# Folding the first LayerNorm of a transformer block into its projections: raw rows transposed, statistics by TensorE, normalised copies by GpSimd

## The chip, the cores and the metric

The kernel runs on one core of one Trainium2 chip. The metric is the device time of one execution in microseconds (us); several executions are taken and their median is compared. Engines are called PE or TensorE (matmul), DVE or VectorE, ACT or ScalarE, POOL or GpSimd, and SP or SyncE, which here only issues DMAs.

## The reference

One pre-LayerNorm attention block and one gated feed-forward block over 2048 rows of 512 features, in bf16:

```python
x = A_x
h = x + _A_ref(_layernorm(x, axis=-1), A_wqkv, A_wo)
h2 = h + _B_ref(_layernorm(h, axis=-1), B_w_gate, B_w_up, B_w_down)

# _A_ref: 32 heads of 16 features, softmax over all 2048 keys
scores = einsum("bhqd,bhkd->bhqk", q, k) * 16 ** -0.5
o = einsum("bhqk,bhkd->bhqd", softmax(scores), v)
# _B_ref: F = 1792
h = sigmoid(x @ w_gate) * (x @ w_up); return h @ w_down
# _layernorm: (x - mean) / sqrt(var + 1e-5), no gain and no offset
```

## The kernel before, in words

The rows are cut into 16 tiles of 128 (`NT`), which form four chunks of 512 rows (`NQC`, `QC`, four tiles `TQ` each). The 32 heads are cut into eight groups of four (`NG`), two groups to a pair (`NP`). `KT[g]` holds the transposed keys of a group, one head to a quadrant of 32 partitions, with a row that is one in each quadrant; `QT[g]` holds the queries of a chunk with a shift in that row, so that scores come out shifted against overflow. `Vaug` holds the values with a constant column for the softmax sums.

**Head.** Raw rows are loaded into `xb`. For each row tile the mean and variance come from DVE (bn_stats, L133, L136) or from ACT (two activations with accumulators, L221 and L223, then two small fixes on DVE). A square root on ACT and a reciprocal on DVE give `rstd`; DVE writes the normalised rows `xn` (L238), TensorE transposes them (L151), DVE or ACT copies the result into `xnT[c]` (L245). Then group 0 is projected (`proj0`, L250) with padded weights `w0p`; keys go to `KT[0]` (L260, L262), their squares through a matmul to a minimum (`kmin`, L297), and with that the shift of the queries (`QT[0]`, L320). Values of eight row tiles are also made here (L155, L182, L184). The instructions are `Task`s with a duration and dependencies; a list scheduler in the program places them on the engines and so writes each engine's order. Task `go` ends the head.

**Loop.** The work of attention is 2048 units of 128 keys by 512 query columns for one head, or by 256 columns for two. Three units (`GU`) form a tile of three PSUM banks, 683 tiles in all. For every tile TensorE makes the scores (L887). ACT takes the exponential of two or three banks (L1227). Where it takes two, DVE takes the third: a tensor_scalar writes an integer code `J` of the scores (L1054), and three further ones add constants to four such codes at a time (`code`, L1074); read as bf16 they sum to the exponential. TensorE multiplies with the values into `acc` (L1028). A second planner with a clock for each of P, A and D decides in which order the three engines do this and which units DVE takes; it never gives DVE a unit in tiles 10 to 19. Between tiles it fits background work from the queue `bg`: values (`prep_v`), keys and queries (`prep_k`, `prep_q`, `prep_q0`), the output projection, the second LayerNorm, and the feed-forward layers of the halves of 256 rows that are finished. `ones_fill` sets a whole `KT[g]` to ones by a DMA, all seven in the head; `spread` then puts the keys over it.

**Tail.** The last half's output projection, LayerNorm and feed-forward layer run after the last exponential.

Each engine runs its instructions in the order written, and waits on semaphores of the others.

Of the kernel before, what the change touches and what calls it, by code (L numbers as in the profile page):

```python
# [26 lines left out]
def kernel(  # L27
# [41 lines left out]
    otp = ctx.enter_context(tc.tile_pool(name="otp", bufs=12))  # L69
# [6 lines left out]
    onecol = const.tile([P, 1], FP32)  # L76
    sel = const.tile([P, 32], BF16)
    selq = const.tile([P, P], BF16)
    ones = const.tile([P, 128], BF16)
    xnT = [const.tile([P, DC, QC], BF16, name=f"xnT{c}") for c in range(NQC)]  # L80
    KT = [const.tile([P, S], BF16, name=f"KT{g}") for g in range(NG)]
# [5 lines left out]
    o2buf = [const.tile([P, QC // 32, 32], BF16, name=f"o2_{i}") for i in range(4)]  # L87
# [6 lines left out]
    w0s = prep.tile([P, 2, DC, 64], BF16)  # L94
    w0p = prep.tile([P, 2, DC * 4, 32], BF16)
# [3 lines left out]
    for c in range(NQC):  # L99
        n = 1 if c == 0 else 2  # L100
        for i in range(0, TQ, n):
            q = (nc.sync, nc.scalar)[(i // n) % 2]
            q.dma_start(out=xb[c][:, i:i + n, :], in_=x_v[:, c * TQ + i:c * TQ + i + n, :])
        if c == 0:
            nc.sync.dma_start(out=w0s[:, 0], in_=wqkv_v[:, :, D:D + 64])
            nc.scalar.dma_start(out=w0s[:, 1], in_=wqkv_v[:, :, 0:64])
# [5 lines left out]
    nc.gpsimd.memset(Vaug[:, :, :, DH:VW], 0.5)  # L112
# [3 lines left out]
    nc.vector.memset(selq[:], 0.0)  # L116
    nc.vector.memset(ones[:], 1.0)
    nc.vector.memset(w0p[:], 0.0)
    nc.vector.tensor_reduce(out=sel[:, 0:8], in_=ident_bf[:].rearrange("p (r k) -> p r k", k=DH),
                            axis=AX.X, op=ALU.max)  # L120
    nc.vector.tensor_reduce(out=onecol[:], in_=ident_bf[:, DH:P:32], axis=AX.X, op=ALU.max)
    nc.vector.tensor_scalar(out=selq[:, DH:P:32], in0=sel[:, 0:8:2], scalar1=-0.5078125,
                            scalar2=None, op0=ALU.mult)
# [4 lines left out]
    def ones_fill(g):  # L128
        nc.sync.dma_start(out=KT[g][:].rearrange("p (c n) -> p c n", n=P),
                          in_=ones[:].rearrange("p (o n) -> p o n", o=1).to_broadcast([P, NT, P]))  # L130
# [42 lines left out]
    def v_mm(ps, t, a=0, b=DC, mm=quarters):  # L173
        for d in range(a, b):
            mm(ps, xnT[t // TQ][:, d, (t % TQ) * P:(t % TQ + 1) * P], wv_sb[:, d, :],
               d == 0, d == DC - 1)

    def v_out(ps, t, act):
        dst = Vaug[:, t, :, 0:DH]
        src = ps.rearrange("p (h d) -> p h d", d=DH)  # L180
        if act:
            nc.scalar.copy(out=dst, in_=src)  # L182
        else:
            nc.vector.tensor_copy(out=dst, in_=src)  # L184

    ps0ctx = ExitStack()
    ps0 = ps0ctx.enter_context(tc.tile_pool(name="ps0", bufs=8, space=PSUM))
# [6 lines left out]
    mvs = [small.tile([P, TQ, nc.vector.BN_AGGR_DIM], FP32, name="mv") for c in range(NQC)]  # L194
    rstds = [small.tile([P, TQ], FP32, name="rstd") for c in range(NQC)]
    kmin = small.tile([P, NQC], FP32, name="kmin", bufs=1)
# [5 lines left out]
    class Task:  # L202
        def __init__(self, name, deps, opts, bank=0, frees=0):
            self.name, self.deps, self.opts, self.bank, self.frees = name, deps, opts, bank, frees
            self.end = None
            tasks[name] = self
# [6 lines left out]
    ACT_STATS = {(0, 1), (1, 2), (1, 3), (2, 1), (2, 3), (3, 1), (3, 2)}  # L213
    CHUNK_FIRST = (5400, 7300, 0, 0)

    def stats_task(c, i):
        src, mv = xb[c][:, i, :], mvs[c][:, i, :]

        def on_act():
            junk = prep.tile([P, D], BF16, name="junk")  # L220
            A.activation(out=junk[:], in_=src, func=ACT.Identity, scale=1.0 / D,  # L221
                         accum_out=mv[:, 0:1])
# [18 lines left out]
    def turn0(c, i):  # L241
        buf["t", c, i] = transpose4(bank0(), buf["xn", c, i])
# [97 lines left out]
    while left:  # L340
        best = None
        for n in left:
            t = tasks[n]
            ends = [tasks[d].end for d in t.deps]
            if None in ends or t.bank > banks:
                continue
# [1057 lines left out]
```

## Time and profile before

| quantity | value |
|---|---|
| median of 3 runs | 828.01 us (826.25 to 828.6) |
| the profiled execution | 826.86 us, of which the span of the profile is 825.1 |
| granted TensorE clock | 0.995 of full speed |
| first exponential of the loop | at 33.55 us |
| tiles in which ACT takes two banks, three banks | 479, 204 |
| units that DVE takes (`J`) | 478 |
| GpSimd instructions in the loop | 1 |

All times in a profile line are in microseconds from the span's start unless marked ns. A line of the timeline gives start, duration, engine, source line, operation, what is written and read, and the form. A line of the groups gives the count after the x, then busy time and the mean ns of one instruction, then the idle time before them and who ended it. An instruction's record is longer than the distance to the next one where the two overlap in the pipeline: a `J` is 0.681 long and follows the one before after 0.61.

### The profile page before, as it was taken

To read this page: it belongs to the slowest core of one execution; us is meant where nothing else is said; L and a number is where in the kernel's file an instruction comes from. 1 tells how busy PE (TensorE), PEld (TensorE's weight loads), DVE (VectorE), ACT (ScalarE), POOL (GpSimd) and SP (SyncE) were. 2 spreads that over 40 slices of the span, in tenths; PEclk is the share of its full clock that TensorE was granted. 3 is DMA by queue.
4 is the path that set the end of the run, shared out by engine and by line. 5 is a ranking of instruction groups with operands and counts; after the bars stand their busy time and mean duration, and the time that the engine had idled before them with its cause. 6 is when DMAs were issued, how large, how long until landed. Compare 5 with 4: busy or idle time off the path is not lost.

```text
span 825.1 us, 34604 instructions
## 1 busy us (share of the span) xinstructions
PE 751.6 (91%) x15255; PEld 364.5 (44%) x15259; DVE 734.3 (89%) x1415; ACT 779.8 (95%) x804; POOL 3.2 (0%) x8
## 2 busy tenths in 40 slices
PE   4889988887889999999999999999899999999988
PEld 2322223333335344555444444553455455455546
DVE  8849999997999999999989899889999889899972
ACT  6899999998999999999989999999999999989972
POOL 1000000000000000000000000000000000000000
PEclk9999999999999999999999999999999999999999
DMA  9700011015001121122022211220132022134110
GB/s 259 130 2 4 16 34 27 13 31 159 8 16 54 42 82 35 47 82 78 16 74 61 64 36 47 81 78 16 45 104 84 28 80 79 48 98 141 43 39 16
DMA packets 90717, 49.47 MB, mean 60 GB/s; under 512 B 20820, under 2 KB 90120, under 8 KB 90568
## 3 DMA queue, kind: packets, MB, share of 16 engines
q1 hardware_dynamic: 88936, 46.15, 21.1%
q8 instruction: 121, 1.98, 0.9%
q10 hardware_dynamic: 1632, 1.11, 0.4%
q14 instruction: 28, 0.23, 0.1%
HBM read 37.62 MB, written 2.10 MB: 48 GB/s over the span
## 4 chain that ended last, share of the span: by engine, by line
ACT 45%; PE 33%; issue 14%; DVE 7%; DMA 0%; ACTq 0%; DVEq 0%
ACT pt L1227 42%; PE pm L160 11%; PE pss L887 9%; PE acc L1028 9%; DVE J L1054 2%; ACT th L759 2%; PE gu L155 2%; DVE code L1074 1%; PE hp L1369 1%; DVE xs L970 1%; PE b L151 0%; DVE st L133 0%; DMA code<-in_A_x_dram 0%; DVE hT L743 0%; DVE xn L238 0%
## 5 line engine op out<-in xcount | busy, mean ns | idle before, releaser
L1227 ACT ACTIVATE pt<-pss 128x1024 bf16<-128x1024 f32 (+1 forms) x683 | 727.8, 1192 | 9.4 <-PE pss L887 6.6
L1054 DVE TENSOR_SCALAR J<-pss 128x512 uint16<-128x512 f32 x478 | 318.1, 681 | 24.5 <-PE pss L887 22.9
L887 PE MATMUL pss<-QT,KT 32*128 32x256 bf16 (+1 forms) x3712 | 269.5, 284 | 50.4 <-ACT pt L1227 39.6
L1074 DVE TENSOR_SCALAR code<-J 128x2048 uint16<-128x2048 uint16 (+3 forms) x387 | 237.4, 643 | 0.3
L1028 PE MATMUL acc<-pt,Vaug 128*17 128x256 bf16 (+1 forms) x2837 | 219.2, 286 | 2.0 <-ACT pt L1227 0.8
L887 PEld LDWEIGHTS <-KT 32*128 32x128 bf16 x3712 | 84.9, 92 | 251.3 <-ACT pt L1227 128.8
L1028 PE MATMUL acc<-code,Vaug 128*17 128x256 bf16 (+1 forms) x2625 | 186.4, 284 | 0.0
L1028 PEld LDWEIGHTS <-Vaug 128*17 128x17 bf16 x6337 | 139.7, 90 | 97.8 <-issue 82.2
L1028 PE MATMUL acc<-J,Vaug 128*17 128x256 bf16 (+1 forms) x875 | 137.2, 284 | 0.1
L160 PE MATMUL pm<-xnT,wgu 128*32 128x256 bf16 x3136 | 117.6, 275 | 1.6 <-DVE hT L743 0.8
L160 PEld LDWEIGHTS <-wgu 128*32 128x32 bf16 x3136 | 77.6, 96 | 27.2 <-issue 23.5
L160 PE MATMUL pm<-wd,hT 128*32 128x512 bf16 x784 | 56.1, 382 | 0.0
L743 DVE SCALAR_TENSOR_TENSOR hT<-th,pm 128x512 bf16<-128x512 f32 x49 | 33.3, 679 | 10.1 <-PE pm L160 8.8
L759 ACT ACTIVATE th<-pm 128x512 f32<-128x512 f32 x49 | 30.7, 626 | 8.3 <-PE pm L160 7.3
L970 DVE STREAM_TRANSPOSE xs<-acc 128x512 f32<-128x512 f32 x32 | 22.8, 712 | 11.5 <-PE acc L1028 11.3
L160 PEld LDWEIGHTS <-hT 128*32 128x32 bf16 x784 | 16.0, 95 | 19.6 <-issue 13.1
L160 PE MATMUL pm<-xnT,wq_sb 128*32 128x512 bf16 x256 | 20.5, 391 | 0.2 <-DVE kr L566 0.2
L160 PE MATMUL pm<-xnT,wk_sb 128*32 128x512 bf16 x256 | 19.7, 383 | 0.1
L151 PE MATMUL b<-ident_bf,xn 128*128 128x128 bf16 x64 | 6.5, 265 | 12.1 <-DVE xn L238 11.4
L160 PE MATMUL pm<-wo_sb,ot 128*32 128x512 bf16 x224 | 17.2, 382 | 0.1
L946 DVE STREAM_TRANSPOSE ot<-o 128x256 bf16<-128x256 bf16 x32 | 13.6, 433 | 0.1
L604 DVE TENSOR_SCALAR sh<-pm,kcol 8x512 bf16<-8x512 f32 x16 | 11.8, 735 | 1.9 <-PE pm L600 1.7
(126 smaller groups left out, 327.2 us busy)
## 6 DMA issues: line engine op xcount, KB each, us to landing
wgu<-in_B_w_gate_dram SPq DMA_DIRECT2D x49, 256.0 KB
wgu<-in_B_w_up_dram SPq DMA_DIRECT2D x49, 256.0 KB
KT<-ones SPq DMA_DIRECT2D x7, 512.0 KB
out_dram<-ob SPq DMA_DIRECT2D x16, 128.0 KB
QT<-qd SPq DMA_DIRECT2D x116, 16.0 KB
KT<-kd SPq DMA_DIRECT2D x28, 64.0 KB
wd<-in_B_w_down_dram SPq DMA_DIRECT2D x1, 1792.0 KB
xr<-in_A_x_dram SPq DMA_DIRECT2D x14, 128.0 KB
```

The lines of the kernel that those rows point to most:

```text
L155: nc.tensor.matmul(ps, lhsT=lhsT, rhs=rhs, start=start, stop=stop)
L160: nc.tensor.matmul(ps[r, :], lhsT=lhsT[:, r], rhs=rhs, start=start, stop=stop, tile_position=(0, 32 * j), skip_group_check=True)
L604: nc.vector.tensor_scalar(out=sh[:], in0=ps2[0:8, :], scalar1=-0.505, scalar2=kcol[p][:, 0:1], op0=ALU.mult, op1=ALU.add)
L743: nc.vector.scalar_tensor_tensor(out=hT[:, 2 * k:2 * k + 2, :].rearrange("p f q -> p (f q)"), in0=th[:], scalar=1.0, in1=ps, op0=ALU.add, ...
L759: nc.scalar.activation(out=th[:], in_=ps, func=ACT.Tanh, scale=0.5)
L887: mm = nc.tensor.matmul(pss[:, ui, a * w:(a + 1) * w], lhsT=KT[hg[a]][32 * j:32 * j + 32, kt * P:(kt + 1) * P], rhs=(QT0[q] if g == 0 and ...
L946: nc.vector.transpose(out=ot[:], in_=o2[:, i * NB:(i + 1) * NB, :] .rearrange("p b r -> p (b r)"))
L970: j = st["acc"] = dve(630, lambda: nc.vector.transpose(out=xs[:].rearrange("p b r -> p (b r)"), in_=acc[:]), Mark(T["P"]))
L1028: nc.tensor.matmul(acc[32 * j:32 * j + VW, a * w:(a + 1) * w], lhsT=Vaug[:, kt, 4 * hg[a] + j, :], rhs=un.ap[:, a * w:(a + 1) * w], start= ...
L1054: first = nc.vector.tensor_scalar(out=J[:, k, :], in0=src, scalar1=128 * SC * LOG2E, scalar2=float(CODE_BASE), op0=ALU.mult, op1=ALU.add)
L1074: nc.vector.tensor_scalar(out=c, in0=j, scalar1=CODE_STEP[i], scalar2=None, op0=ALU.add)
L1227: ex = nc.scalar.activation(out=pt[:, lo:lo + wa, :], in_=pss[:, lo:lo + wa, :], func=ACT.Exp, scale=SC)
```

## The change

The normalised row is `rstd * (x - mean)`. If every column of a weight is centred (its mean over the 512 features is taken off), the raw row times the centred weight, times `rstd`, is the same projection, and no mean has to be taken off a row. The change uses this:

- Raw rows are transposed as they land, into `xr[c]`, without statistics. Beside the 128 columns of each row tile stand 64 centred key weights of group 0 and a column of 1/512.
- One matmul of `xr` with itself and these columns (`gram`, four steps for a row tile) gives the Gram matrix, whose diagonal is the sum of squares, the keys of group 0, and the row means. DVE takes the diagonal (product with the identity, then a reduction); ACT squares the mean; variance, square root, reciprocal follow.
- Keys, queries and values of group 0 are scaled by `rstd` on eviction (`scale0`, `vscale0`), transposed by TensorE, and evicted into `KT[0]` and `QT[0]`. Key squares are summed on ACT and DVE from the untransposed keys.
- Column means of weights come from a matmul with a matrix of 1/512 (`wmean`). Group 0's weights are centred by DVE, and copied to the other chunks by GpSimd; `wv`, `wk` and `wq` are centred by GpSimd (`center`), four instructions each.
- GpSimd makes the normalised transposed copies `xnT[c]` (`normalise`), four instructions for each chunk; the row factors get there through DRAM and a broadcast (`spread0`, four writes and four reads on SyncE). The later projections use these copies.
- Values of the other 28 heads are made in the loop for all 16 row tiles, from raw rows, and scaled on eviction; none is made in the head.
- Chunk 3 too takes groups 0 and 1 with 512 columns; DVE may take units in tiles 10 to 19; `ones_fill` moves into `prep_k`; the raw transposed rows of chunks 0 to 2 lie in the `KT` of pairs 1 to 3, the row factors of chunks 0 and 1 in `KT[1]`, until these are filled. All later rows of x are issued by SyncE; a third block of weights (`w0s[:, 2]`) is loaded.

The core of the diff:

```diff
-    for c in range(NQC):
-        n = 1 if c == 0 else 2
-        for i in range(0, TQ, n):
-            q = (nc.sync, nc.scalar)[(i // n) % 2]
...
+    nc.scalar.dma_start(out=w0s[:, 2], in_=wqkv_v[:, :, 2 * D:2 * D + 64])
+    for c in range(1, NQC):
+        for i in range(0, TQ, 2):
+            nc.sync.dma_start(out=xb[c][:, i:i + 2, :], in_=x_v[:, c * TQ + i:c * TQ + i + 2, :])
...
+    nc.gpsimd.memset(Vaug[:, :, :, DH:VW], 0.5)
...
-    def v_out(ps, t, act):
...
+    def v_out(ps, t):
+        nc.vector.tensor_scalar(out=Vaug[:, t, 4:H, 0:DH],
+                                in0=ps[:, 0:D - 64].rearrange("p (h d) -> p h d", d=DH),
+                                scalar1=rstd[:, t:t + 1], scalar2=None, op0=ALU.mult)
...
     def turn0(c, i):
-        buf["t", c, i] = transpose4(bank0(), buf["xn", c, i])
+        buf["t", c, i] = transpose4(bank0(), xb[c][:, i, :])
...
+    def gram(c, i):
+        if not i:
+            buf["g", c] = ps0g.tile([P, TQ, 2 * P], FP32, name="g0")[:]
         for d in range(DC):
-            E.matmul(ps, lhsT=w0p[:, which, 4 * d:4 * d + 4, :], rhs=xnT[c][:, d, :],
+            E.matmul(buf["g", c][:, i, 0:P + 65], lhsT=xr[c][:, d, i, 0:P], rhs=xr[c][:, d, i, 0:P + 65],
                      start=(d == 0), stop=(d == DC - 1))
...
+    def diagonal(c, a, b):
...
+        V.tensor_tensor(out=g[:, a:b, :], in0=buf["g", c][:, a:b, 0:P],
+                        in1=ident_bf[:].rearrange("p (o t) -> p o t", o=1).to_broadcast([P, b - a, P]),
+                        op=ALU.mult)
+        V.tensor_reduce(out=buf["ss", c][:, a:b], in_=g[:, a:b, :], axis=AX.X, op=ALU.add)
...
+    def center0():
+        V.tensor_tensor(out=xr[0][:, :, :, P:P + 64],
...
+        for c in range(1, NQC):
+            nc.gpsimd.tensor_scalar(out=xr[c][:, :, :, P:P + 64], in0=xr[0][:, :, :, P:P + 64],
+                                    scalar1=1.0, scalar2=0.0, op0=ALU.mult, op1=ALU.add)
...
+    def center(ps, w, copy):
+        m = prep.tile([P, D], FP32, name="wmean", bufs=2)
+        copy(out=m[:], in_=ps)
+        for d in range(DC):
+            nc.gpsimd.tensor_tensor(out=w[:, d, :], in0=w[:, d, :], in1=m[:], op=ALU.subtract)
+
+    def normalise(c):
+        for d in range(DC):
+            nc.gpsimd.tensor_tensor(out=xnT[c][:, d, :].rearrange("p (i t) -> p i t", t=P),
+                                    in0=xr[c][:, d, :, 0:P], in1=R[c], op=ALU.mult)
...
     def prep_v(t):
-        yield pe(2, pm_new())
+        yield pe(2, pm_new(), WC["v"])
...
     def prep_k(p, groups=(0, 1)):
+        for a in groups:
+            sp_issue(1, T["P"])
+            ones_fill(2 * p + a)
...
-            yield pe(2, pm_new())
+            yield pe(2, pm_new(), XN[c], WC["k"])
...
-        if (len(tl) == GU and not 10 <= n < 20 and len(jq) < 2
+        if (len(tl) == GU and len(jq) < 2
```

## The prediction, before the changed kernel was run

> **What bounds the kernel now.** I read the page first: the share of each engine, then the sums by stage, then the head in order of time.
>
> ```profile
> PE 751.6 (91%) x15255; PEld 364.5 (44%) x15259; DVE 734.3 (89%) x1415; ACT 779.8 (95%) x804; POOL 3.2 (0%) x8
> ```
>
> ScalarE (ACT) is the fullest engine, and GpSimd (POOL) does nothing. An average over the span hides three stages, so the second view is the busy time in three windows: the head up to the first exponential, the attention loop, the tail.
>
> ```profile
> 0.00:33.50 33.50, 19.74 (x125) 10.95 (x127) 27.89 (x90) 24.20 (x57) 2.90 (x7) 1.00 1.08 235
> 33.50:798.50 765.00, 709.50 (x14929) 338.04 (x14928) 697.29 (x1309) 747.84 (x734) 0.30 (x1) 1.00 0.19 54
> 798.50:825.10 26.60, 22.34 (x205) 15.55 (x204) 9.09 (x17) 7.81 (x13) 0.00 (x0) 0.99 0.05 16
> ```
>
> After each window's length come PE, weight loads, DVE, ACT, POOL, then granted clock and DMA. In the loop ACT is idle for 17 of 765 us: whatever delays it there is lost for good. In the head no engine is full; VectorE (DVE, 27.9 of 33.5 us) is nearest, and the chain that ended last runs there through DVE's statistics, normalisation and reductions. The third view is the order of time around the first exponential.
>
> ```profile
> 31.69 0.75 DVE L320 TENSOR_SCALAR QT<-b,kfull 128x512 bf16<-128x512 f32 x1
> ...
> 32.35 0.68 DVE L184 CAST Vaug<-b 128x512 bf16<-128x512 f32 x1
> 33.09 0.61 PE L887 MATMUL pss<-QT,KT 32*128 32x512 bf16 x6 [1.14 <-DVE Vaug L184]
> ...
> 33.55 1.02 ACT L1227 ACTIVATE pt<-pss 128x1024 bf16<-128x1024 f32 x1 [1.89 <-PE pss L887]
> ```
>
> The shifted queries are done at 32.44, then the scores wait out one more value eviction and the loop starts at 33.55. The change rebuilds everything before this line and puts 28 two-input GpSimd instructions behind it (TensorTensor rows; the program shows them). So I read what the trace knows of GpSimd beside VectorE.
>
> ```profile
> 1.25 2.26 POOL L112 MEMSET Vaug<- 128x512 bf16 x1
> 1.62 0.23 DVE L119 TENSOR_REDUCE sel<-ident_bf 128x8 bf16<-128x128 bf16 x1
> ...
> 1.76 0.14 DVE L121 TENSOR_REDUCE onecol<-ident_bf 128x1 f32<-128x4 bf16 x1
> 1.88 1.66 DVE L122 TENSOR_SCALAR selq<-sel 128x4 bf16<-128x4 bf16 x1
> ```
>
> The tensor_scalar touches 4 elements per partition and takes 1.66 us; small ones elsewhere take 0.16 to 0.17 (nt, nv). It ends at 3.54, 0.03 us after the memset at 3.51. Reductions beside the same memset ran at their usual length. Where a DVE instruction reads and writes SBUF alone, it seems to wait for the running GpSimd instruction. The loop's code instructions are of that kind.
>
> ```profile
> L1054 DVE TENSOR_SCALAR J<-pss 128x512 uint16<-128x512 f32 x478 | 318.1, 681 | 24.5 <-PE pss L887 22.9
> ...
> L1074 DVE TENSOR_SCALAR code<-J 128x2048 uint16<-128x2048 uint16 x327 | 214.2, 682 | 0.2
> ```
>
> A J reads PSUM; a code is SBUF to SBUF and does four times the elements in the same time. The one GpSimd instruction of the loop (ones, 0.30 us at 35.18) ran beside a J of 0.69, the usual length.
>
> **The head, part by part.** Removed: 9 bn_stats of 0.66, 7 pairs of ACT statistics (0.63 each plus a 0.19 accumulator read), 16 normalisations of 0.41, 5 squares, 4 reductions of 0.69, 9 value evictions of 0.6 to 0.7, and the wait for statistics before the first transpose, which now starts on raw rows. The seven 512 KB fills of KT also leave the head's DMA. Added: Gram products and centred weights.
>
> First piece. x lands at 3.87 (the first bn_stats starts there). The third matmul group on TensorE is the mean of three w0s blocks, and all later transposes queue behind it. SyncE waited for w0s until 5.95; a third block of 64 KB makes it about 6.3 (estimate). Mean 0.44, then the centring of 1024 elements, 1.2 us (twice the 0.61 spacing of J): 8.0. Four Gram groups and three transpose groups follow at 0.42 each (24 transposes took 2.74, so 0.46 per four; 16 took 1.44): 10.9.
>
> Second piece, DVE's queue from the first diagonal to QT: 6 instructions of 512 elements at 0.68 and 4 halves at 0.42 (diagonals), 11 of 256 at 0.42 (scaled keys, queries, values, sums), 18 small at 0.165, the key minimum 0.25, QT 0.75. That is 4.1 + 1.7 + 4.6 + 3.0 + 1.0 = 14.4, so 25.3. I add 1.0 for square roots on ACT (0.29 each, mostly behind a key sum) and for one small instruction caught behind a GpSimd weight copy. QT is done at 26.3; 0.1 for the handover and 0.46 from scores to exponential (33.09 to 33.55) give a first exponential at 26.9. TensorE's queue from 8.0 (12 transpose groups, 16 Gram, 4 query, 5 key and query turns, two means) gives about 25 as well; ACT's, 11 copies of 0.59, 4 evictions, small work and a 1.28 table load, gives 22. Bounds: 24.4 if all instructions overlap as J does (0.681 long, 0.61 apart), 28.6 if DVE is filled to 86% as between 20 and 33 us now. **Gain 6.65, from 4.9 to 9.1.** The raw rows' row factors go to DRAM and back; GpSimd needs them only after 27 us, and the SyncE work behind (wo) is not due before tile 16. The KT fills now stand on SyncE ahead of each pair's key spread; the first waits until GpSimd has read the row factors out of KT1 (24 + 12 × 1.2 = 38 us, with the price below), and behind it stands only the spread of keys that are projected after 54. I cost both at nothing.
>
> **The loop.** Of the 683 exponentials 481 instead of 479 cover two banks and 202 instead of 204 three; starts 33.55, 34.47, 35.38 give 0.915 for two, and 46.40, 47.73 give 1.33 for three: 2 × 0.415 = **0.83 less**. Sixteen value evictions of 28 heads replace eight of 32 in the loop, about 5 us more DVE, and the hole in which DVE took no exponentials (tiles 10 to 19; DVE busy 10.4 of 20 us between 40 and 60) now takes it. I cost that at nothing because the two-bank count says the work is spread, not shrunk; without that hole DVE has no cover left in the first 30 tiles.
>
> GpSimd's price per 512-element product: no row has it. Below, 0.30 for 128 elements (ones) × 4 = 1.2; above, the 512-element memset with a stride, 2.26. I take 1.2, the row with contiguous runs as here. The Trainium skill (GPSIMD Engine Reference, section 3.1) gives 4497 ns for 2048 fp32 elements of a two-input add, by which a quarter would be 1.12 (estimate); the sum would not move.
>
> The centring of wv can start when ACT has copied its mean, about 24. While the first 24 products run (wv, four normalised chunks, wk), the DVE order holds 13 codes. By the selq row each waits for the rest of a product, 0.6 on average, less the 0.3 that a two-bank tile leaves DVE beside a J (0.915 − 0.61): 13 × 0.3 = **3.9 lost**. Bounds: 0, as J beside ones showed, and 15.6 for a whole product each time.
>
> Sum on the profiled execution: 826.86 − 6.65 − 0.83 + 3.9 = 823.3. That execution lies 1.15 below the median of 828.01, so the forecast for the median is **824.4**.
>
> **Rivals.** *GpSimd is late, and TensorE waits* (ends slower). Keys of group 1 are projected after tile 27 of scores, in order on TensorE, so a late wk stops scores and then ACT. Twenty of the first 27 exponentials cover two banks: 18.3 + 9.3 = 27.6, so wk is due about 54.5; at 1.2 the chain from 24 ends at 52.8, with 13 codes of 0.62 in between at 60.8, which the codes' own delay nearly matches. Every 0.1 us per product adds 2.4. It cancels the gain of 7.5 at 1.58 per product; halfway between the bounds, 1.73, it waits 11 us: 831.5 for the median. At 2.26 it would be 844. For: two inputs on one engine that no row has shown. Against: the contiguous row.
>
> *The codes pay in full.* No tile hides a wait: 13 × 0.6 = 7.8, and the gain is gone, 828.3. For: DVE was busy 19.2 of 20 us between 80 and 100. Beside it stands the Trainium skill (GPSIMD Engine Reference, section 8), which has GpSimd share its SBUF interfaces with VectorE and contend with a two-port mode; by that rule every code counts. The selq row agrees; no run here yet shows two engines in a long contest.
>
> *No contest at all.* 828.01 − 7.5 = 820.5, if selq was slow for another cause.
>
> *It doesn't do what it says.* The statistics' longer chain (Gram, diagonal, square root, reciprocal, scale, turn, evict) serialises and the first exponential stays at 31: 828.5. Against: the three queues worked out above end within 3 us of each other.
>
> **How the numbers follow.** A measurement of this kernel tells 0.3% from no change (2.5 us, as the three runs spread 2.35). Forecast 0.42, late GpSimd 0.27, codes in full 0.13, no contest 0.13, head not shorter 0.05. Faster: the forecast's larger part (0.39) and no contest, 0.52. Same: the codes' full price, the rest of the forecast's spread, less what turns slower: 0.15. Slower: late GpSimd with the upper parts of the others, 0.33. Range: 817.5 (no contest and the head 3 us shorter) to 834 (GpSimd at about 1.85 per product), which leaves out the two ends.
>
> **What would show it.** First exponential at 26.9: right step one. GpSimd products near 1.2 us, and codes beside them of 1.0 to 1.3 instead of 0.68: right step three. TensorE idle before pm of wk_sb: the slower rival. I am wrong if the first exponential is past 30, if codes keep 0.68, or if the loop from first to last exponential grows by more than 7.

## The result, and the profile after

The changed kernel takes **839.93 us** (median of 4 runs, 837.12 to 842.24) against 827.45 (4 runs, 826.25 to 828.6): a ratio of 1.0149, 95% interval 1.0112 to 1.0187. It is slower by 12.5 us where 3.6 less were forecast; the forecast's range ended at 834. The profiled execution took 838.88, its span 837.1, 12.0 more than the span before.

The engines' shares, then the three windows of the prediction (after each length PE, weight loads, DVE, ACT, POOL, granted clock, DMA share, GB/s):

```profile
PE 758.0 (91%) x15095; PEld 366.5 (44%) x15099; DVE 745.1 (89%) x1421; ACT 771.2 (92%) x781; POOL 44.7 (5%) x50
```

```profile
0.00:32.90 32.90, 16.83 (x178) 13.75 (x179) 22.96 (x69) 14.57 (x34) 16.93 (x28) 0.94 0.44 126
32.90:803.40 770.50, 712.41 (x14631) 334.01 (x14631) 710.18 (x1329) 746.28 (x731) 27.75 (x23) 0.98 0.23 59
803.40:837.10 33.70, 28.72 (x300) 18.78 (x290) 12.01 (x24) 10.39 (x17) 0.00 (x0) 1.00 0.08 25
```

The head lost work (DVE 22.96 instead of 27.89, ACT 14.57 instead of 24.20) and hardly any time. The loop from first to last exponential grew from 761.0 to 770.5, the rest behind it from 30.6 to 33.7. So 12.0 = −0.6 (head) + 9.5 (loop) + 3.1 (tail).

DVE's order of time at the end of the head:

```profile
25.59 0.15 DVE L299 TENSOR_TENSOR r<-rstd 128x4 f32<-128x4 f32 x1
...
25.87 1.12 DVE L264 SCALAR_TENSOR_TENSOR var<-ss,m 128x4 f32<-128x4 f32 x1
...
28.15 1.09 DVE L299 TENSOR_TENSOR r<-rstd 128x4 f32<-128x4 f32 x1
29.27 1.09 DVE L300 TENSOR_TENSOR kk<-kk,r 128x16 f32<-128x16 f32 x1
```

An instruction of four elements takes 0.15 us, and the same one 1.09 as soon as GpSimd runs (its value centring, from 25.80 to 30.34). Three of them cost 2.8 us on the chain that sets QT.

GpSimd's order of time in the loop, and SyncE's queue beside it:

```profile
30.29 4.39 POOL L371 TENSOR_TENSOR xnT<-KT,KT 128x512 bf16<-128x512 bf16 x4
41.69 5.72 POOL L371 TENSOR_TENSOR xnT<-KT,KT 128x512 bf16<-128x512 bf16 x4 [7.02 <-DMA KT<-rows]
...
64.35 4.82 POOL L371 TENSOR_TENSOR xnT<-xr,R 128x512 bf16<-128x512 bf16 x4 [6.00 <-DMA R<-rows]
69.13 4.50 POOL L367 TENSOR_TENSOR wk_sb<-wk_sb,wmean 128x512 bf16<-128x512 bf16 x4
```

```profile
25.64 2.64 SPq L340 DMA_DIRECT2D rows<-rstd  x1
37.14 0.33 SPq L341 DMA_DIRECT2D KT<-rows  x1
37.56 0.39 SPq L340 DMA_DIRECT2D rows<-rstd  x1
48.17 0.33 SPq L341 DMA_DIRECT2D R<-rows  x1
```

```profile
SPq L341 <- DMA rows<-rstd: 36.9, 4, 10.2
```

GpSimd works 4 to 6 us and waits 5.7 to 7 for the next row factors. Each read (L341) stands on SyncE behind its own write (L340) and ahead of the next write. Each waits 8 to 10 us until its write of 512 single numbers has landed, so the reads are issued 11 to 12 us apart, and GpSimd can start on the last row factors only at 64.35. The waits of TensorE put a price on it (total, times, longest):

```profile
PE pm L185 <- POOL wk_sb L367: 6.4, 2, 5.9
```

The key weights `wk` are centred behind the last of these passes, and TensorE needs them for the keys of group 1. Counted from 0, exponential 26 starts at 63.65 and exponential 27 at 73.24 (before: 64.77 and 65.67). ScalarE stands idle for 8.14 us ahead of it; this jump is the largest single loss of the loop:

```profile
73.24 4.41 ACT L1369 ACTIVATE pt<-pss 128x1024 bf16<-128x1024 f32 x4 [8.14 <-PE acc L1159]
```

### The profile page after: what moved, and what is told of

It reads as the page before. It is cut to its first block, busy times and chain, and to the rows that moved or that the text cites. A ratio compares the mean times of both kernels' runs of the same rounds, so it can differ in the third digit from the quotient of the medians.

```text
span 837.1 us, 34314 instructions
## 1 busy us (share of the span) xinstructions
PE 758.0 (91%) x15095; PEld 366.5 (44%) x15099; DVE 745.1 (89%) x1421; ACT 771.2 (92%) x781; POOL 44.7 (5%) x50
## 4 chain that ended last, share of the span: by engine, by line
ACT 41%; PE 35%; issue 12%; DVE 6%; DMA 2%; POOL 2%; ACTq 0%; DVEq 0%; POOLq 0%
ACT pt L1369 38%; PE pm L185 12%; PE acc L1159 10%; PE pss L1020 10%; DVE J L1185 2%; ACT th L892 2%; PE gu L180 1%; DMA rows<-rstd 1%; POOL xnT L371 1%; PE hp L1513 1%; DVE code L1205 1%; DVE xs L1101 1%; DMA w0s<-in_A_wqkv_dram 1%; DMA R<-rows 1%; PE g L246 0%
## 5 line engine op out<-in xcount | busy, mean ns | idle before, releaser
L1205 DVE TENSOR_SCALAR code<-J 128x2048 uint16<-128x2048 uint16 (+2 forms) x390 | 242.2, 650 | 0.3
L1020 PEld LDWEIGHTS <-KT 32*128 32x128 bf16 x3584 | 83.1, 92 | 247.6 <-ACT pt L1369 135.0
L1159 PEld LDWEIGHTS <-Vaug 128*17 128x17 bf16 x6104 | 134.8, 90 | 99.6 <-issue 81.4
L185 PEld LDWEIGHTS <-wgu 128*32 128x32 bf16 x3136 | 77.9, 96 | 28.5 <-issue 25.1
L876 DVE SCALAR_TENSOR_TENSOR hT<-th,pm 128x512 bf16<-128x512 f32 x49 | 33.2, 678 | 9.7 <-PE pm L185 6.9
L886 DVE SCALAR_TENSOR_TENSOR ob<-pm,h 128x512 bf16<-128x512 f32 x14 | 9.6, 685 | 4.5 <-PE pm L185 4.1
```

Source lines behind the costliest of these rows:

```text
L185: nc.tensor.matmul(ps[r, :], lhsT=lhsT[:, r], rhs=rhs, start=start, stop=stop, tile_position=(0, 32 * j), skip_group_check=True)
L876: nc.vector.scalar_tensor_tensor(out=hT[:, 2 * k:2 * k + 2, :].rearrange("p f q -> p (f q)"), in0=th[:], scalar=1.0, in1=ps, op0=ALU.add, ...
L886: nc.vector.scalar_tensor_tensor(out=ob[:], in0=ps, scalar=0.5, in1=fstate.pop((h, i))[:], op0=ALU.mult, op1=ALU.add)
L1020: mm = nc.tensor.matmul(pss[:, ui, a * w:(a + 1) * w], lhsT=KT[hg[a]][32 * j:32 * j + 32, kt * P:(kt + 1) * P], rhs=(QT0[q] if q < NQC and ...
L1159: nc.tensor.matmul(acc[32 * j:32 * j + VW, a * w:(a + 1) * w], lhsT=Vaug[:, kt, 4 * hg[a] + j, :], rhs=un.ap[:, a * w:(a + 1) * w], start= ...
L1205: nc.vector.tensor_scalar(out=c, in0=j, scalar1=CODE_STEP[i], scalar2=None, op0=ALU.add)
```

## The experiments

One table first. "First exp." is where the first exponential starts, "26 → 27" the distance between the starts of these two, "loop" from the start of the first to that of the last, "tail" the rest behind it; these four are of the profiled execution. The time is the median of all executions, with the ratio to the kernel before in the same set of runs. Runs e4 and e11 start from the kernel before, all others from the changed kernel. In the kernel before the rows read 33.55, 0.9, 761.0, 30.6.

| run | first exp. | 26 → 27 | loop | tail | time | ratio (95%) |
|---|---|---|---|---|---|---|
| changed kernel | 32.91 | 9.6 | 770.5 | 33.7 | 839.93 | 1.0149 (1.0112 to 1.0187) |
| e1 rows ahead | 32.31 | 2.3 | 768.7 | 33.6 | 837.65 | 1.0122 (1.0086 to 1.0157) |
| e2 staging tile | 32.49 | 10.3 | 769.5 | 33.7 | 837.09 | 1.0108 (1.0076 to 1.0140) |
| e3 both | 31.92 | 2.8 | 770.2 | 33.5 | 835.01 | 1.0094 (1.0062 to 1.0126) |
| e4 before + 28 products | 33.58 | 0.9 | 775.8 | 30.6 | 840.86 | 1.0158 (1.0128 to 1.0188) |
| e5 no GpSimd in the loop (part of the work left out) | 32.44 | 2.3 | 758.3 | 33.3 | 824.55 | 0.9963 (0.9946 to 0.9979) |
| e7 products on VectorE | 32.78 | 7.1 | 773.2 | 33.1 | 838.91 | 1.0118 (1.0087 to 1.0149) |
| e8 centring held back | 29.03 | 2.3 | 767.1 | 33.5 | 832.64 | 1.0048 (1.0028 to 1.0068) |
| e9 factor at the PSUM read | 29.59 | 0.9 | 775.1 | 33.2 | 838.86 | 1.0132 (1.0115 to 1.0149) |
| e10 e9 + 9 matmuls | 29.26 | 0.9 | 773.3 | 33.3 | 838.48 | 1.0117 (1.0091 to 1.0143) |
| e11 before + 28 one-input | 33.56 | 0.9 | 764.6 | 30.6 | 829.64 | 1.0012 (0.9998 to 1.0026) |
| e12 e10, two buffers | 29.49 | 0.9 | 778.3 | 33.2 | 843.94 | 1.0211 (1.0187 to 1.0234) |
| e13 e10, old order | 30.05 | 2.3 | 770.9 | 33.2 | 837.57 | 1.0130 (1.0101 to 1.0159) |
| e14 e13, factors resident | 29.65 | 2.3 | 763.4 | 33.1 | 831.09 | 1.0050 (1.0033 to 1.0068) |

**e1, the writes ahead of the reads.**

```diff
     def spread0(c):
         nc.sync.dma_start(out=rows[c].rearrange("i t -> t i"), in_=rstd[:, c * TQ:(c + 1) * TQ])
-        nc.sync.dma_start(out=R[c].rearrange("p i t -> p (i t)"),
-                          in_=rows[c].rearrange("i t -> (i t)").partition_broadcast(P))
...
+    for c in range(NQC):
+        read0(c)
     for c in range(NQC):
         normalise(c)
```

> The changed kernel with one edit: the four writes of the row factors to DRAM are issued on SyncE ahead of the four reads, where the changed kernel issues write, read, write, read. Everything else keeps its order. Theory A (the serial round trips through DRAM made GpSimd late, and with it the key weights): the reads land within some 10 us of each other instead of 11 us apart, the last near 40 us instead of 59 to 60, the key weights are centred by 55 instead of 69, TensorE's wait of 6 us before the key projection and the 7.6 us jump at exponential 27 are gone, and the time falls from 839.9 to 829 to 832. Rival B (GpSimd's own work is the bound: 24 products of 1.1 to 1.4 us and their contest with VectorE): the normalising passes run one behind the other but the jump at exponential 27 keeps more than 5 us, and the time is 836 or more. Rival C (the loop makes the loss up again later, since something further on is the bound): the jump goes, but the exponentials from index 100 on stand within 2 us of where they stood in the changed kernel, and the time stays at 838 or more.

The jump went (9.6 to 2.3), so it was the trips through DRAM. But the time fell by only 2.3, and the ranges of the two versions overlap (836.38 to 838.36 against 837.12 to 842.24). The groups of DVE between 33 and 75 us say where the rest went:

```profile
L1189 DVE TENSOR_SCALAR J<-pss 128x512 uint16<-128x512 f32 x22 | 14.6, 680 | 0.7 <-PE pss L1024 0.6
L1209 DVE TENSOR_SCALAR code<-J 128x2048 uint16<-128x2048 uint16 x11 | 13.3, 1227 | 0.0
L1209 DVE TENSOR_SCALAR code<-J 128x1536 uint16<-128x1536 uint16 x3 | 3.8, 1267 | 0.0
```

The same two forms of the code in the changed kernel, in the same stretch:

```profile
L1205 DVE TENSOR_SCALAR code<-J 128x2048 uint16<-128x2048 uint16 x10 | 10.1, 1035 | 0.0
L1205 DVE TENSOR_SCALAR code<-J 128x1536 uint16<-128x1536 uint16 x3 | 1.6, 544 | 0.0
```

With the writes ahead, GpSimd's first product with a row factor starts later (39.57 instead of 30.29), but all of them run to 71 without a gap, `wk` is ready at 66.0 instead of 73.6 and first used at 70.2, and codes take 1.23 instead of 0.68; in the changed kernel, with its gaps, ten of them took 1.04 and those of 1536 elements their usual 0.54. Summed over codes and small instructions VectorE waits 10.8 us in e1 (11 × 0.55 + 3 × 0.72 + 3 × 0.52 + 3 × 0.35) and 5.5 in the changed kernel. One wait was bought with another. The part of Theory A on the jump held, the part on the time did not. The total lies between those of Rival B (836 or more) and Rival C (838 or more), but neither holds whole: the jump went, against B, and exponential 100 stands 2.6 earlier than in the changed kernel, where C allowed 2.

**e2, a staging tile.** GpSimd copied group 0's centred weights out of the tile into which ScalarE also copies raw rows; now it reads a tile of its own.

```diff
+        V.tensor_tensor(out=cw0[:], in0=w0s[:, 0], ... op=ALU.subtract)
...
-            nc.gpsimd.tensor_scalar(out=xr[c][:, :, :, P:P + 64], in0=xr[0][:, :, :, P:P + 64],
+            nc.gpsimd.tensor_scalar(out=xr[c][:, :, :, P:P + 64], in0=cw0[:]... .to_broadcast(...),
```

> The changed kernel with one edit: the centred key weights of group 0 are written to a small tile of their own, and GpSimd copies them from there into the three padded tiles, so GpSimd no longer reads from the tile into which ScalarE and VectorE copy the raw transposed rows (one more VectorE instruction of 256 elements). Theory A (the copy of a raw transposed tile by ScalarE, the one with 7.4 us of idle ahead of it put down to GpSimd, waited for a shared tile): that copy comes some 4 us earlier, the Gram matmuls of the first chunk run through, the first exponential comes at 28.5 to 30 instead of 32.9. The total moves by 0 to 4, since the key weights still wait for the rows from DRAM: 836 to 840. Rival B (the late first weights or VectorE's own queue set the head): the copy comes earlier, the first exponential stays past 32, the total moves by less than 1.

ScalarE's copy came at 9.84 instead of 12.55, and the first exponential only 0.4 earlier. For the head Rival B: the copy did not hold it by 4 us; most of that gap was idle time of an engine with slack. The total is 2.8 lower, more than Rival B's 1, but with ranges that overlap (835.09 to 837.74 against 837.12 to 842.24).

**e3, both edits.**

> Both edits together: the four writes of the row factors ahead of the reads, and the staging tile for the centred key weights of group 0. Theory A (two separate faults, one in the head of 4 us and one at the key projection of 8 us): first exponential at 28.5 to 30, no jump at exponential 27, time 826 to 829; what is left of the forecast's difference is VectorE's codes beside GpSimd (some 4 us) and 3 us in the tail. Rival B (the early head only makes the key projection wait longer for GpSimd): first exponential early, but a wait of TensorE for the key weights takes its place, time within 2 us of the version with the early writes alone.

Neither: first exponential 31.92, time 2.6 under e1 (835.01 against 837.65, their ranges overlap). Two faults were mended and 7.5 us still missing, most of it between exponentials 10 and 27 (28.5 us there, 21.9 before).

**e4, GpSimd beside the loop, measured by itself.** The kernel before with 28 products behind exponential 60; nothing uses their output.

```diff
+        if n == 60:
+            for i in range(28):
+                nc.gpsimd.tensor_tensor(out=pjunk[:, i % 4, :], in0=xnT[3][:, i % 4, :], in1=pfac[:], op=ALU.mult)
```

> The kernel before, with 28 GpSimd products added in the loop near 100 us, 512 elements on 128 partitions each, bf16 by float32 to bf16, like those of the changed kernel, with an output that nothing uses: the contest of GpSimd with VectorE measured by itself. Theory A (an SBUF-to-SBUF instruction of VectorE waits until the GpSimd instruction that runs has ended): the codes from SBUF in the stretch of some 32 us go from a mean near 0.68 to 1.0 or more, those that read PSUM stay as they are, and the exponentials behind the stretch stand 3 to 8 us later; the time is 831 to 835. Rival B (VectorE has enough slack there, or there is no contest): the codes keep 0.68 to 0.75, and the time stays within 1.5 us of the kernel before.

Theory A held and was too small. GpSimd first, then DVE between 102 and 141 us:

```profile
L1279 POOL TENSOR_TENSOR pjunk<-xnT,pfac 128x512 bf16<-128x512 bf16 x27 | 36.9, 1404 | 0.0
```

```profile
L1077 DVE TENSOR_SCALAR code<-J 128x2048 uint16<-128x2048 uint16 x12 | 16.2, 1365 | 0.0
L1057 DVE TENSOR_SCALAR J<-pss 128x512 uint16<-128x512 f32 x16 | 10.4, 675 | 0.0
```

A code takes twice its 0.68, a J (which reads PSUM) nothing more. Exponential 100 stands 14.8 later than before, of which 1.2 was there ahead of the products, and the time is 13.4 more: 0.48 us for each product of 1.40. The extra length of DVE's instructions adds up to about as much, 13.2 between 95 and 140 us and 14.2 up to 142. So next to nothing of it is hidden.

**e5, the loop without GpSimd.**

```diff
-            nc.gpsimd.tensor_tensor(out=xnT[c][:, d, :]..., in0=xr[c][:, d, :, 0:P], in1=R[c], op=ALU.mult)
+            nc.sync.dma_start(out=xnT[c][:, d, :]..., in_=xr[c][:, d, :, 0:P])
...
-        for d in range(DC):
+        for d in range(DC if w is wv_sb else 0):
             nc.gpsimd.tensor_tensor(out=w[:, d, :], in0=w[:, d, :], in1=m[:], op=ALU.subtract)
```

> The version with both edits (early writes, staging tile), with GpSimd's work in the loop left out: the 16 normalising products are replaced by DMA copies of the raw transposed rows, and the 8 centring products of the key and query weights of the later groups are left out, as are the row factors' trips through DRAM. Left out of the computation: the normalisation of keys and queries of all groups but the first. Theory A (GpSimd's products cost VectorE 10.8 us of waiting between 33 and 75 us in the version with early writes, and TensorE's low clock at 54 to 66 us there follows from it): codes from SBUF back at 0.68, exponential 27 about 7 us earlier than in that version, granted clock 1.00 from 40 us on, time 827 to 829, which is the kernel before less 1.6 in the head and plus 3 in the tail. Rival B (the loop's start is slow because of the new small VectorE work for queries and values, or because the clock is low from 25 us on): exponential 27 stays more than 4 us later against exponential 0 than in the kernel before, and the time stays above 832.

```profile
L1213 DVE TENSOR_SCALAR code<-J 128x2048 uint16<-128x2048 uint16 x15 | 9.9, 685 | 0.0
```

Theory A, and more: codes back at 0.685, the loop 758.3, the time 824.55. This version leaves out the normalisation of the later groups' keys and queries, and with the products go the row factors' trips that they wait for. TensorE's order is instruction for instruction that of the changed kernel, so the two loops can be laid over each other: the changed kernel loses 3.2 us up to exponential 26, 7.2 in the jump to 27, 1.3 up to 40, and 0.4 in all that follows. Of its 12.2 us, 7.2 are lateness: in e1 the order of the DMAs alone takes that jump away. The other 5.0 I put down to the contest, since VectorE's instructions are 5.5 longer there. Not separated from it is TensorE's clock, which was 0.50 from 66.3 to 76.6 us in the changed kernel, around the wait for `wk`, and 1.00 in e5.

**e7, the same 24 products on VectorE**, spread over 40 to 65 us.

```diff
-            nc.gpsimd.tensor_tensor(out=xnT...
+            V.tensor_tensor(out=xnT...   # queued one by one as VectorE work
```

> The version with both edits, with the 16 normalising products and the 8 centring products of key and query weights on VectorE instead of GpSimd, spread over the stretch from 40 to 65 us. Theory A (a GpSimd product costs VectorE 0.49 us of waiting, as measured with 28 of them, and 0.42 us if VectorE does it itself): the time is that of the version on GpSimd less 0 to 3 us, 832 to 835; GpSimd saves VectorE nothing. Rival B (the waits are mostly in VectorE's slack, and GpSimd does take work off): VectorE's 10 us come on top, and the time is 838 or more.

```profile
L378 DVE TENSOR_TENSOR xnT<-KT,KT 128x512 bf16<-128x512 bf16 x8 | 5.4, 687 | 0.0
```

A product with a float32 factor takes 0.69, not 0.42: 16.5 us of VectorE for 24, and Rival B's time. By the instruction, GpSimd's 0.48 is the better price. The two times do not decide it: their ranges overlap (835.36 to 841.0 here, 834.85 to 837.43 for e3), the planner ordered the loop anew, and the products, spread to 66 us, make their own jump of 7.1 at exponential 27.

**e8, the value centring held back** until the shift of the first queries is known (a one-number GpSimd instruction reads `kfull`, then come the four products).

```diff
+    nc.gpsimd.tensor_scalar(out=buf["wv"][:, 0:1], in0=kfull[:], scalar1=0.0, scalar2=buf["wv"][:, 0:1], ...)
+    subtract(wv_sb, buf["wv"])
```

> The version with both edits, with GpSimd's centring of the value weights (4 products, 4.5 us) held back until the shift of the first scores is known, so that it runs in the first microseconds of the loop and not beside the last small VectorE instructions of the head. Theory A (three small instructions of the head took 1.1 instead of 0.16 us because each waited for a GpSimd product): they go back to 0.16 to 0.18, the first exponential comes 2.5 to 3 us earlier, at 29, and the loop gives back 1.5 to 2: time 833 to 834.5. Rival B (the head is set by the chain through ScalarE and TensorE): the small instructions get short, but the first exponential moves by less than 1.

```profile
25.09 0.15 DVE L264 SCALAR_TENSOR_TENSOR var<-ss,m 128x4 f32<-128x4 f32 x1
...
26.40 0.15 DVE L299 TENSOR_TENSOR r<-rstd 128x4 f32<-128x4 f32 x1
26.59 0.17 DVE L300 TENSOR_TENSOR kk<-kk,r 128x16 f32<-128x16 f32 x1
...
28.03 0.48 DVE L446 TENSOR_SCALAR QT<-b,kfull 128x512 bf16<-128x512 bf16 x1
```

Theory A: all three short, the first exponential 2.9 earlier than in e3, 2.4 in the time. Of the head's forecast gain of 6.65, 4.5 is there.

**e9, no product at all for the row factors.** VectorE reads each projection from PSUM anyway; it multiplies there.

```diff
-                nc.vector.tensor_copy(out=kd[:, c * QC:(c + 1) * QC], in_=ps)
+                nc.vector.tensor_tensor(out=kd[:, c * QC:(c + 1) * QC], in0=ps, in1=R[c]..., op=ALU.mult)
```

> The version with the held-back value centring, with GpSimd's 16 normalising products gone and nothing put in their place on an engine: the raw transposed rows go to their tiles by DMA, and the row factor is multiplied in where VectorE reads a projection from PSUM anyway (the cast of 0.68 us becomes a product of a PSUM tile with the row factors). The 8 centring products of key and query weights run on VectorE with a mean in bf16. Theory A (the whole loss in the loop was VectorE waiting for GpSimd): the product from PSUM takes 0.69, a centring product 0.42 instead of the 0.69 that one with a float32 input took, so VectorE has 3.4 us more than in the version without GpSimd's work in the loop, and 2 us of waits beside the value centring; against that the first exponential is 3 us earlier: 822 to 826, faster than the kernel before. Rival B (what the version without this work gained came from leaving the reads of the row factors and their DMA traffic out, or the key projection waits for the row factors): a wait of over 2 us at the first key projection, 828 or more.

Up to exponential 27 Theory A holds (it starts at 60.2, in no run before as early; the product takes 0.69, a centring product 0.42). Then the loop falls behind e5 in steps at exponentials 92, 135, 155, 170 and later, and its last exponential is 14 us behind e5's. So the time is one that Rival B allows, but not by the wait at the first key projection that it named. The planner made a new order for these durations, and the steps can come from that or from the row factors' reads; e12 to e14 take this up.

**e10, nine matmuls more** in the idle places at the end of the head.

> The same with nine more matmuls of 512 columns at the end of the head, with an output that nothing uses, where TensorE stands idle for 0.5 to 1.1 us at a time before the last transposes. Theory A (TensorE's granted clock of 0.50 from 30 to 34 us and 0.78 from 34 to 40 follows from its idle time between 24 and 30 us, and costs the first exponentials something): the clock from 30 to 40 us rises to over 0.9, the stretch from exponential 0 to 10 shrinks from 11.6 towards 10.6 us, time 0.5 to 1.5 us less than without. Rival B (the low clock costs nothing, as ScalarE and VectorE bound that stretch): the clock rises and exponentials 0 to 10 keep their spacing; time the same within 0.5.

The windows of e9 and of e10 from 30 us on (PE busy, granted clock, DMA share, GB/s):

```profile
30.00:34.00 4.00, 4.00 (x33) 0.50 1.52 66
```

```profile
30.00:34.00 4.00, 3.14 (x36) 1.00 1.59 43
```

The clock went from 0.50 to 1.00, exponentials 0 to 10 from 11.1 to 10.2 us: Theory A for that stretch. In the total 0.4 of it is to be seen, far within the spread and within the 0.5 of Rival B.

**e11, GpSimd with one input.** As e4, with a scale by one number per partition.

```diff
-                nc.gpsimd.tensor_tensor(out=pjunk[:, i % 4, :], in0=xnT[3][:, i % 4, :], in1=pfac[:], op=ALU.mult)
+                nc.gpsimd.tensor_scalar(out=pjunk[:, i % 4, :], in0=xnT[3][:, i % 4, :], scalar1=pfac[:, 0:1], ...)
```

> The kernel before with 28 GpSimd instructions near 100 us as in the earlier run, but each scales its tile by one number per partition and so reads a single tensor from SBUF instead of two; the output is not used. Theory A (VectorE waits for any GpSimd instruction that runs): the codes from SBUF go to 1.0 us or more as long as GpSimd is busy, and the loss is 0.3 to 0.4 us for each microsecond of GpSimd, as with the products. Rival B (only GpSimd instructions with two inputs from SBUF make VectorE wait): codes keep 0.68, the time stays within 1.5 us of the kernel before.

```profile
L1077 DVE TENSOR_SCALAR code<-J 128x2048 uint16<-128x2048 uint16 x15 | 11.1, 750 | 0.0
```

```profile
L1279 POOL TENSOR_SCALAR pjunk<-xnT,pfac 128x512 bf16<-128x512 bf16 x27 | 51.5, 1924 | 0.0
```

Rival B by the time (1.5 more, an interval that holds no change), but the contest is not gone. In the profiled execution codes of 2048 elements take 0.75 and those of 1536 elements 0.79 instead of 0.55, and VectorE's instructions are 3.0 us longer in all, against 13 to 14 in e4. GpSimd waits too: its instruction takes 1.56 us where no code runs beside it (at 107.60, 110.69 and 131.46), 1.92 on average, and up to 3.39. So the form is slower by itself than the product of e4 (1.15 at its shortest) and still costs VectorE less.

**e12, two buffers again** for query tiles and squares, row factors in bf16.

> The version with the row factor multiplied in at the read of PSUM and the nine extra matmuls, changed in one respect: the query tiles written from PSUM and their squares have two buffers each again, as in the changed kernel (that version had one each, to make room for the row factors of the later chunks), and the room comes from row factors in bf16 and one output buffer. Theory A (what that version lost came in steps at exponentials 92, 135, 155 and 170, 10 us in all against the version without GpSimd's work in the loop, because VectorE's write of a query tile waited for the DMAs that still read the one buffer): the steps go, exponential 200 comes within 2 us of where it is in the version without GpSimd's work, first exponential at 29.5, time 822 to 827. Rival B (the planner's order, changed by the new work on VectorE, makes the steps): they stay, time 834 or more.

Rival B in the main: the steps at 92, 135 and 155 stayed. The one at 167 to 171 shrank (from exponential 155 to 171 e12 falls 0.9 us further behind e5, e10 5.6), so the single buffer may have had a part in it. A new stop of 6.8 us in the first ten exponentials came on top, in which TensorE, VectorE and ScalarE all stood:

```profile
ACT pt L1409 <- remote: 6.8, 1, 6.8
```

The DMA engines then show a busy share of 1.6 to 1.8 and move 25 to 28 GB/s, with 2-byte row factors among their writes. What exactly stopped the engines is not settled.

**e13, the old order of work.** The planner is given the old durations, so that VectorE's and TensorE's orders are those of e8 (and e5).

> The version with the row factor multiplied in at the read of PSUM, the nine extra matmuls and one buffer each for query tile and square, with the order of work in the loop that the planner made for the version with the held-back value centring: the planner is told the old durations and due times (GpSimd's products, though they are gone), and the new instructions stand in the places of the old ones. Theory A (the 11 to 17 us that the two versions before lost in the loop against the version without GpSimd's work came from another order of work, which the planner made from other due times): the loop takes 758 us from first to last exponential as in the version without GpSimd's work, plus 3.4 for the centring on VectorE, 2 beside the value centring and up to 3 of waits for row factors: last exponential at 791 to 796, time 824 to 829. Rival B (the new instructions and their DMA reads cost it, whatever the order): the loop takes over 768 us, time 834 or more.

```profile
DVE qd L760 <- DMA Rq<-rows: 9.5, 2, 6.4
```

Laid over e5 the loop now loses time in three places: 4.5 us between exponentials 15 and 25 (the eight centring products, 3.3 us of VectorE in two blocks, and what queues behind them), 7.4 at 125 and 3.2 at 270. The last two are these two waits, 6.4 and 3.1: VectorE's product stands until the row factors are read again from DRAM, with its codes queued behind. By its numbers this is Rival B (loop over 768, time over 834). The scattered steps are gone with the old order, so the new order had made them; but the two waits for the reads stand in their place, and the time moved by only 0.9 from e10, within the spread.

**e14, row factors resident in bf16.**

> The last version with the row factors kept in SBUF in bf16 for the whole loop instead of being read again from DRAM for each chunk's queries (GpSimd rounds them, four copies with a single input near 40 us); order of work and everything else the same, but for one output buffer. Theory A (of the 10.2 us that the last version stood behind the version without GpSimd's work at its last exponential, 10.6 came at two places, 7.4 at exponential 125 and 3.2 at 270, where VectorE's product waited for the row factors' read): both steps go, last exponential at 791 to 793, time 825 to 828, which is the kernel before or up to 0.4% faster. Rival B (the steps came from the single buffer of the query tile): they stay, time 835 or more.

The steps at 125 and 270 are gone (a new one of 1.4 stands at 134), the last exponential is at 793.1 (e13: 800.9): Theory A for the place, not for the time. The profiled execution is the shortest of the ten, 828.07; they go up to 835.0 and their median is 831.09. It beats the changed kernel by 9 us and is 0.5% behind the kernel before.

## Why the prediction was wrong, step by step

Three steps failed: the row factors' trips were costed at nothing, the head's gain was put at 6.65 and came out at 0.64, and the tail had no term. Term by term, on the profiled execution: the forecast's 823.3, then 6.0 for the head, 7.2 for the jump that stood in no term, 1.1 for the codes, −1.8 for the loop's own order and 3.1 for the tail, which stood in no term either, make 838.9; measured were 838.88.

**The head (forecast 26.9, measured 32.91).** The first exponential past 30 was named as a sign of being wrong, and so it is. It lies outside the forecast's bounds of 24.4 and 28.6 as well, of which the upper one is 29.2 by its own working (14.4 at 86% is 16.7, behind 10.9, with 1.56 to follow). Three parts, from the two traces. (1) "First piece … 10.9": the first diagonal starts at 14.50. The first weights landed at 7.25 instead of 6.3, their mean took 0.80 instead of 0.44, the centring ended at 9.37 instead of 8.0; then the seven groups and their copies took 5.1 us instead of 2.9 (4.3 in e3, without the shared tile; a Gram group alone lasts 0.65 where I had put 0.42). That is 3.6 us, 0.8 of them the shared tile, the rest of price and not of mechanism. The same Gram matmul follows the one before after 0.16 us up to 10.9 us and after 0.08 from 13.2 on; the profile's clock column says 1.00 for both stretches, so what halves the rate is open. (2) "one small instruction caught behind a GpSimd weight copy", 1.0 in all with the square roots: three were caught, behind the value centring. From first diagonal to QT it took 17.7 instead of 15.4; with the centring held back (e8) 14.8. So the sum over DVE's queue was right, and the allowance for instructions caught behind GpSimd was too small. (3) 0.2 at the handover.

**"GpSimd needs them only after 27 us … I cost both at nothing."** The step that failed most. I had read the row factors' DMAs as free because no engine waits for them in the head, and looked at what they delay on SyncE, not at how long one trip lasts and that four stand in a row. The trips followed one another 11 to 12 us apart, GpSimd stood still for 19 us between its passes, wk came at 73.6 instead of 52.8, and TensorE waited: 7.2 us in the jump. The other half of "both", the KT fills, came late as well (the first at 64.78 instead of 38), but no wait of TensorE, VectorE or ScalarE is put down to them.

**GpSimd's product, 1.2.** Measured 1.15 to 1.35 by group, 1.26 on average: within the bounds, and by the forecast's own sum (24 × 0.06 = 1.4 later than 52.8) no cause of the delay. The Trainium skill's figure (GPSIMD Engine Reference, section 3.1), an estimate of 1.12 from 4497 ns, fits the undisturbed ones.

**The codes' wait, 3.9.** It came out at 5.0 (up to exponential 26, from 27 to 40, and the rest), near the forecast by luck: GpSimd stood idle for 19 of the 48 us. By the forecast's own schedule, products without gaps, it is the 10.8 of e1: the price 0.3 for a code, which let the tile's slack absorb half, is too low; e4 shows that next to nothing is absorbed. "The codes pay in full", 0.13, described the mechanism; its 7.8 was still short.

**The loop's own order, −0.83.** e5 shows −2.7, and the tail, for which the forecast had nothing, gives 2.7 of it back: one feed-forward product of 56 matmuls that the planner had no room for stands ahead of the last value matmuls (3.19 us at 803.50). That it costs those 3 us is read from the order, not tested.

**The rivals.** "GpSimd is late, and TensorE waits" had the place right (wk_sb, and its line was the sign named) and the mechanism wrong: its price was the product, and at the measured 1.26 it would have cost nothing. "No contest" is refuted. "It doesn't do what it says" had the head right (31 or later, measured 32.91) at a chance of 0.05; the cause was not the serial chain alone that it named, but the prices and the three caught instructions above. Of the rivals' times the late one's were nearest (831.5, and 844 at its upper price), and none held both GpSimd effects at once.

With both GpSimd effects out, e5 takes 824.55, next to the forecast's 824.4. That is chance: its head is 5.5 us later than forecast, its codes wait for nothing, and part of the computation is left out. With the centring held back as well it would be some 821 (an estimate: the first exponential of e8 is 3.4 before that of e5). No run did it with the whole computation: in e14 the centring on VectorE takes 4.3 us back and the last exponential is 2.4 behind e5's.

## What to carry to other kernels

Before work goes to an idle GpSimd, ask which of VectorE's instructions read and write SBUF alone: where VectorE is full, each microsecond of a two-input GpSimd product cost 0.34 us of the loop (e4), and packing the products without gaps made VectorE wait longer, not less (10.8 us in e1, 5.5 in the changed kernel). A small DMA that nothing waits for yet still has a length: write the trip's duration and its place in the queue into the sum, and if four such trips exist, issue the four writes before the first read. By the instruction, the cheapest place for a factor was one that reads PSUM anyway (e9: 0.69 for 0.68), though no whole version with it beat the kernel before. And when a planner writes the order of work, compare at the old order first (e13): its new choices move the losses about, and what the new instructions cost can't be read from the total.

## What the runs showed of the hardware

- **Who waits for whom depends on the GpSimd form.** Two inputs: codes 1.37 instead of 0.68, products 1.40 (e4). One input: codes 0.75, GpSimd 1.92 on average where 1.56 was its length with no code beside it (e11). Instructions that read PSUM kept their length in both (a J 0.675 and 0.671). The Trainium skill (SBUF — State Buffer, section "SBUF: two separate sides") has a pair of ports that VectorE and GpSimd hold for a whole instruction, whoever starts first; by that rule a one-input GpSimd instruction should block codes as well, and the trace agrees only in part: three codes of 0.67 run wholly inside a GpSimd instruction of 3.39 us (e11, from 115.86), and both engines get longer.
- **A write of 512 single float32 numbers** (2 KB) took 8 to 10 us to land here (changed kernel, from the end of its issue to the read behind it); with four of them issued ahead of the reads, GpSimd's products start at 39.57 and run to 71 without a wait (e1).
- **TensorE's granted clock fell to 0.50** from 28.8 to 35.6 us in the changed kernel, after 3.4 us (25.4 to 28.8) in which TensorE was busy for 0.79 us, and again from 66.3 to 76.6, around the wait for wk. Nine matmuls that nothing uses kept it at 1.00 from 24 to 40 us (e10). The Trainium skill (TensorE: Matmul & The Clock Gate, Part 1) has the clock at half after an idle window of about 3.4 us; the trace agrees in part: the clock fell, though TensorE did not stand idle for the whole of those 3.4 us.
- **Runs of one kernel spread with that clock**: e14's ten run from 828.07 (clock 0.990) to 835.0 (0.982), the kernel before beside them from 825.5 (0.998) to 830.17 (0.990). Which drives which is not shown.
